# One PSUM tile per matmul bank, a transpose bank of its own, and batch 2 transposed on TensorE

## The chip, the core and the metric

The kernel runs on one core of a Trainium2 chip, as one launch. Of the core's engines it uses TensorE (PE: matmuls, with the weight loads shown apart as PEld), VectorE (DVE), ScalarE (ACT), a little GpSimd (POOL), and SyncE (SP), whose queue issues most DMAs. Matmul results go to PSUM, which has eight banks of 128 partitions x 512 float32; everything else stands in SBUF. The metric is the device time of one execution in microseconds. A profile is one execution of its own, with its own time.

## What is computed

```
def _attn_ref(q, k, v):                      # (8 batches, 8 heads, 576 tokens, 64)
    def phi(x, c, s):
        r = np.maximum(x, 0.0)
        return np.concatenate([r * c, r * s], axis=-1)
    q_p, k_p = phi(q, cos_w, sin_w), phi(k, cos_w, sin_w)   # cos, sin of the token's place
    kv = np.einsum('bhsf,bhsd->bhfd', k_p, v)
    z = np.sum(k_p, axis=2)
    num = np.einsum('bhsf,bhfd->bhsd', q_p, kv)
    den = np.einsum('bhsf,bhf->bhs', q_p, z)[..., None] + 1e-06
    return num / den
def _moe_ref(x, w_in, w_out):                # x (4608, 512), w_in (512, 2048), w_out (2048, 512)
    h = x @ w_in
    return (h * np.cos(h)) @ w_out
```

The attention's output, heads side by side, is x.

## The kernel before

**Attention, batch by batch.** `load` brings k, q and v of a batch into `raw` (km, qm, vm; one buffer each, so the next batch's load waits until this batch's was read). `prep` makes the two features of k and q with ReLU and a scale, one half on DVE, one on ACT (L236, L233), for five tiles t of 128 tokens; the fifth is half of one and is shared by two batches. `cast_v` makes v float16 (L249). `kv` sums kv and z of all heads into the two banks of the PSUM tile `ATT` (L257) and copies them to `kvz`. q must be transposed (feature by token): `q_pe` does it on TensorE into a PSUM bank, from which DVE or ACT copies it to `qT` (L288, L294, L292); `q_dma` does it with a DMA transpose from the SP queue (L298). Batches 0 and 1 take the first, the others the second way. `num` multiplies qT by kvz (L319); DVE takes the denominators (`den`), their reciprocals (`rec`) and the product x (L324, L327, L329). x is transposed in turn, by `x_pe` (L348, copied by ACT, L352) for the four whole tiles of batches 0 and 1 or by `x_dma` (L358), into `xT` or, for the shared tiles, `xR`.

**The two layers, in nine chunks of 512 tokens.** Chunk c is the whole tiles of batch c; chunk 8 is xR. `layer1` fills a PSUM bank with 4 (chunks 0 and 1: 8 of half the width) matmuls, 16 banks a chunk (L412, L395). For each bank ACT writes cos into `ch` (L368, one of four buffers) and DVE multiplies bank and ch into `gT` (L370). `layer2` sums 16 matmuls for each of four token tiles in a bank of M2 (L436); ACT copies it to `ost` (L448) and a DMA writes it out.

**PSUM.** The eight banks are four tiles of two banks: M1P[0], M1P[1] for layer 1 in turn, M2P for layer 2, and ATT. The early transposes and numerators borrow them as `PAIRS`. The profile and the orders below strip or number these: M is a tile of M1P or M2P.

**What sets the order.** Nothing is issued where it is written. Each step is recorded by `pl.add` with its engine, the time it is planned to occupy it, a due time and the keys that it reads and writes (a key is one bank, such as ("M1", 0)). `Plan.run` lists the steps by planned start and the functions are called in that order; each engine then runs its own instructions in that order. A DMA step occupies SP for its planned time and one shared wire for its bytes over its rate. The waits between engines are not the plan's: the framework adds them, and, as the orders below show, from the tiles that an instruction touches.

Of the kernel before, what the change touches and what calls it, by code (L numbers as in the profile page):

```python
# [11 lines left out]
ALU = mybir.AluOpType  # L12
# [87 lines left out]
def kernel(  # L100
# [41 lines left out]
    def sb(name, shape, dt=F16):  # L142
# [60 lines left out]
    def load(b, nm, due, hs=(slice(0, H),)):  # L203
        m, n = raw[nm], b % 2
        for i, h in enumerate(hs):
            five, four = tokens(src[nm][b][h])
            part = [(nm, hh) for hh in range(H)[h]]

            def go5(h=h, five=five):
                nc.sync.dma_start(out=blocks(m, n)[:, h], in_=five)  # L210

            def go4(h=h, four=four):
                nc.sync.dma_start(out=blocks(m, 1 - n)[:, h, 0:NT, :], in_=four)
# [3 lines left out]
            pl.add("SP", 0.62, 0, due, go4, (), [(x, 1 - n) for x in part],  # L217
                   dma=(nb * NT / 1e3, 330.0))
# [77 lines left out]
    def q_dma(b, t, due):  # L296
        dst, dkey = qdst(b, t)
        pl.add("SP", 0.62, 0, due, lambda: nc.sync.dma_start(  # L298
            out=dst, in_=qp[:, t].rearrange("p h g d -> p (h g d)"), transpose=True),
            [("qp", t, g, h) for g in range(2) for h in range(H)], [dkey],  # L300
            dma=(262.0, 200.0))

    xcount = [0]

    def num(b, t, due, pair=AT):
        A, *ak = pair
        n = xcount[0] % NX
        xcount[0] += 1
        parts = [(qdst(b, t)[0], kvz[b % 2])]
        rd = [qdst(b, t)[1]] + [("kvz", b % 2, i) for i in range(2)]  # L310
        if t == NT:
            parts.insert(0, (qT4[1 - b % 2], kvz[1 - b % 2]))
            rd += [("qT4", 1 - b % 2)] + [("kvz", 1 - b % 2, i) for i in range(2)]

        def mm():
            for h in range(H):
                hb, hh = divmod(h, HB)
                for i, (a, z) in enumerate(parts):
                    nc.tensor.matmul(  # L319
                        A[:, hb, hh * D1:(hh + 1) * D1], lhsT=a[:, h, :], rhs=z[:, h, :],  # L320
                        start=(i == 0), stop=(i == len(parts) - 1))
        pe(H * len(parts), MMA, due, mm, rd, ak)
        N = A[:, :, 0:HB * D1].rearrange("p b (h d) -> p b h d", h=HB)
        dve(0.08, due, lambda: nc.vector.tensor_scalar_add(  # L324
            out=den[n].rearrange("p (b h) -> p b h", b=2), in0=N[:, :, :, D], scalar1=1e-6),
            ak, [("den", n)])
        dve(0.12, due, lambda: nc.vector.reciprocal(out=rec[n], in_=den[n]),  # L327
            [("den", n)], [("rec", n)])
        dve(0.62, due, lambda: nc.vector.tensor_tensor(  # L329
            out=x16[n].rearrange("p (b h) d -> p b h d", b=2), in0=N[:, :, :, 0:D],  # L330
            in1=rec[n].rearrange("p (b h) -> p b h", b=2).unsqueeze(3).broadcast_to((P, 2, HB, D)),
            op=ALU.mult), ak + [("rec", n)], [("x16", n)])
        return n
# [7 lines left out]
    def x_pe(b, t, n, bank, key, eng, due):  # L341
# [8 lines left out]
        pe(NCT, MMT, due, mm, [("x16", n), "ID"], [key])  # L350
# [24 lines left out]
    def layer1(c):  # L375
# [29 lines left out]
        for j in range(NJT):  # L405
            m = m1n[0] % 4
# [17 lines left out]
    def layer2(c):  # L424
        G = gT[c % 2]
        NQ = 4
        for t in range(NT):
            m = m2n[0] % 2
# [29 lines left out]
            def put(dst, s, keys, q=nc.sync, eng="SP", nb=256.0):  # L458
                pl.add(eng, 0.62, 0, due + 1.0, lambda: q.dma_start(out=dst, in_=s), keys, [],
                       dma=(nb, 330.0))  # L460
# [7 lines left out]
            else:  # L468
                for n in range(2):
# [49 lines left out]
    def attention(b):  # L519
        T = start[b]  # L520
        if b == 0:
# [38 lines left out]
        for t in range(NT + 1):  # L560
# [10 lines left out]
        for t in ts:  # L571
            tt = T - 14 + 1.5 * t if t < NT else T
            if early and t < NT:
                pair = PAIRS[(0, 1, 3, 0)[t]]
                n = num(b, t, tt, pair)
                x_pe(b, t, n, pair[0][:, 0, :], pair[1], "ACT", tt)
            else:
                n = num(b, t, tt)
                x_dma(b, t, n, tt + 1)

    def late_q0():
        for g in range(2):
            prep(0, "q", NT, g, "DVE", 24, after=[("g", 0, 0, 0)])
        q_pe(0, NT, ATT[:, 0, :], ("ATT", 0), "ACT", 25)
# [48 lines left out]
```

## Time and profile before

| | |
|---|---|
| time, median of 3 runs (lowest, highest) | 350.78 us (350.75, 351.85) |
| the profiled execution | 350.4 us, of which the span from first to last instruction is 348.6 |
| granted TensorE clock, mean | 0.992 |
| DMA | 53.87 MB in 80217 packets, mean 155 GB/s |

The profile's rows are read so. A timeline row has start and length in us, engine, line of the source, operation, output<-inputs, how many instructions it merges, and in brackets the idle time before it and what ended it. A grouped row has, behind the count, busy us, the mean ns of one, then the idle us just before such instructions and what ended most of it. An instruction's length runs from its start to its last result; those that follow one another on an engine overlap, so a series can take less than the sum. A row of the chain of waits has start, length and what: the work that ended last, followed back from the end.

### The profile page before, as it was taken

The page shows a single profiled execution, that of the slowest core. Times are in us where ns is not written, and L with a number is a line of the kernel's source. Part 1 is how long each engine was busy: PE and PEld are TensorE (multiplying, and loading weights), DVE is VectorE, ACT ScalarE, POOL GpSimd, SP SyncE. Part 2 cuts the span into 40 slices and gives each one's busy share as a digit, 9 for nine tenths or more (in the row PEclk, how much of TensorE's full clock was granted, in tenths as well). Part 3 has the DMA queues.
Part 4 walks back from the last instruction along what each step waited for, and adds up shares of the span by engine and source line. Part 5 has one row for each costly group of instructions (what it writes and reads, how often), then busy time and mean ns, then how long its engine had stood idle before and what let it go on. Part 6 is the DMA issues. An engine that isn't in the chain of part 4 may idle for free.

```text
span 348.6 us, 5319 instructions
## 1 busy us (share of the span) xinstructions
PE 292.8 (84%) x2032; PEld 154.1 (44%) x2032; DVE 181.0 (52%) x387; ACT 179.2 (51%) x290; POOL 7.9 (2%) x19
## 2 busy tenths in 40 slices
PE   0478899676888779878988998999999999999983
PEld 0466646565543335433433453545444444444331
DVE  2646546967844667566666663643464333333300
ACT  2845558777553664564755665344433443443311
POOL 0430000000000000000000000000000000000000
PEclk9989999999999999999999999999999999999998
DMA  6999958999999989798494641561041010101111
GB/s 211 246 224 210 220 194 275 318 286 222 227 223 273 330 141 280 232 208 203 135 270 137 107 107 30 127 116 60 1 117 68 16 60 0 62 0 60 60 62 60
DMA packets 80217, 53.87 MB, mean 155 GB/s; under 512 B 48832, under 2 KB 77760, under 8 KB 80192
## 3 DMA queue, kind: packets, MB, share of 16 engines
q1 hardware_dynamic: 75520, 49.17, 53.3%
q0 software_dynamic: 4224, 4.19, 7.3%
q8 instruction: 16, 0.26, 0.3%
q10 hardware_dynamic: 448, 0.17, 0.2%
q14 instruction: 9, 0.07, 0.1%
HBM read 36.74 MB, written 9.44 MB: 132 GB/s over the span
## 4 chain that ended last, share of the span: by engine, by line
PE 57%; ACT 19%; DVE 12%; issue 6%; DMA 4%; SPq 0%; DVEq 0%; ACTq 0%
PE M L436 28%; PE M L412 20%; ACT ch L368 10%; DVE gT L370 10%; PE M L395 5%; DMA qm<-in_q_dram 4%; ACT ost L448 4%; ACT qp L233 2%; PE ATT L257 2%; PE ATT L319 1%; DVE x L329 1%; ACT V L246 1%; PE M L288 1%; ACT kp L233 1%; ACT qT L292 0%
## 5 line engine op out<-in xcount | busy, mean ns | idle before, releaser
L370 DVE TENSOR_TENSOR gT<-M,ch 128x512 f16<-128x512 f32 x144 | 98.2, 690 | 110.1 <-ACT ch L368 53.9
L368 ACT ACTIVATE ch<-M,PIH 128x512 f32<-128x512 f32 x144 | 96.6, 686 | 112.5 <-DVE gT L370 83.3
L436 PE MATMUL M<-w_out_sb,gT 128*128 128x512 f16 x576 | 141.0, 379 | 11.4 <-ACT ost L448 10.9
L412 PE MATMUL M<-xT,w_in_sb 128*128 128x512 f16 x384 | 94.7, 378 | 11.7 <-DVE gT L370 9.0
L436 PEld LDWEIGHTS <-gT 128*128 128x128 f16 x576 | 54.6, 97 | 76.7 <-issue 18.1
L412 PEld LDWEIGHTS <-w_in_sb 128*128 128x128 f16 x448 | 43.2, 97 | 68.2 <-issue 21.1
L395 PE MATMUL M<-xT,w_in_sb 128*128 128x256 f16 x256 | 30.4, 272 | 8.3 <-DVE gT L370 6.5
L448 ACT ACTIVATE ost<-M 128x512 f32<-128x512 f32 x35 | 20.6, 592 | 32.1 <-PE M L436 32.1
L395 PEld LDWEIGHTS <-w_in_sb 128*128 128x128 f16 x256 | 24.6, 97 | 13.1 <-issue 6.8
L233 ACT ACTIVATE kp<-km,CS 128x512 f16<-128x512 f32 x40 | 26.2, 712 | 4.9 <-DMA km<-in_k_dram 4.9
L233 ACT ACTIVATE qp<-qm,CS 128x512 f16<-128x512 f32 x39 | 26.2, 713 | 2.7 <-DMA qm<-in_q_dram 2.7
L236 DVE TENSOR_SCALAR kp<-km,CS 128x512 f16<-128x512 f32 x40 | 16.6, 481 | 11.3 <-DMA km<-in_k_dram 6.7
L329 DVE TENSOR_TENSOR x<-ATT,rec 128x512 f16<-128x512 f32 x30 | 20.6, 688 | 0.6
L319 PEld LDWEIGHTS <-qT 128*128 128x128 f16 x320 | 15.0, 101 | 10.1 <-issue 4.5
L236 DVE TENSOR_SCALAR qp<-qm,CS 128x512 f16<-128x512 f32 x41 | 18.1, 476 | 1.8 <-DMA qm<-in_q_dram 1.8
L288 PE MATMUL M<-IDENT,qp 128*128 128x128 f16 x72 | 6.3, 258 | 12.2 <-ACT qp L233 12.2
L412 PE MATMUL M<-xR,w_in_sb 128*128 128x512 f16 x64 | 16.4, 379 | 0.0
L319 PE MATMUL ATT<-kvz,qT 128*128 128x65 f16 x272 | 13.7, 195 | 2.0 <-DVE x L329 2.0
L249 DVE CAST V<-vm 128x512 f16<-128x512 f32 (+1 forms) x42 | 14.2, 382 | 0.0
L257 PE MATMUL ATT<-V,kp 128*128 128x65 f16 x320 | 11.8, 194 | 1.7 <-DVE V L249 1.0
L257 PEld LDWEIGHTS <-kp 128*128 128x128 f16 x320 | 11.1, 98 | 3.8 <-DVE V L249 1.2
L288 PEld LDWEIGHTS <-qp 128*128 128x128 f16 x80 | 6.2, 117 | 13.0 <-ACT qp L233 12.4
(38 smaller groups left out, 58.7 us busy)
## 6 DMA issues: line engine op xcount, KB each, us to landing
out_dram<-ost SPq DMA_DIRECT2D x32, 256.0 KB, 2.8
km<-in_k_dram SPq DMA_DIRECT2D x8, 640.0 KB, 5.3
qm<-in_q_dram SPq DMA_DIRECT2D x8, 640.0 KB, 5.7
km<-in_k_dram SPq DMA_DIRECT2D x8, 512.0 KB, 6.1
qm<-in_q_dram SPq DMA_DIRECT2D x8, 512.0 KB, 6.7
vm<-in_v_dram SPq DMA_DIRECT2D x6, 640.0 KB, 4.9
vm<-in_v_dram SPq DMA_DIRECT2D x6, 512.0 KB, 5.9
w_in_sb<-in_moe_w_in_dram POOLq DMA_DIRECT2D x4, 512.0 KB, 9.4
```

Of the source, the lines that this page charges most:

```text
L233: act(0.2 + 0.37 * f, due, lambda: nc.scalar.activation(out=out_, in_=in_, func=AF.Relu, scale=sc), rd, wr)
L236: dve(0.09 + 0.28 * f, due, lambda: nc.vector.tensor_scalar(out=out_, in0=in_, scalar1=0.0, scalar2=sc, op0=ALU.max, op1=ALU.mult), rd, wr)
L257: nc.tensor.matmul(ATT[:, hb, hh * D1:(hh + 1) * D1], lhsT=kp[:, t, h].rearrange("p g d -> p (g d)"), rhs=V1[b % 2][:, t, h, :], start=(t ...
L288: nc.tensor.matmul(ps[:, h, :], lhsT=qp[:, t, h].rearrange("p g d -> p (g d)"), rhs=IDENT, is_transpose=True)
L319: nc.tensor.matmul(A[:, hb, hh * D1:(hh + 1) * D1], lhsT=a[:, h, :], rhs=z[:, h, :], start=(i == 0), stop=(i == len(parts) - 1))
L329: dve(0.62, due, lambda: nc.vector.tensor_tensor(out=x16[n].rearrange("p (b h) d -> p b h d", b=2), in0=N[:, :, :, 0:D], in1=rec[n].rearra ...
L368: act(0.59, due, lambda: nc.scalar.activation(out=ch[c], in_=bank, func=AF.Sin, bias=PIH, scale=1.0), [key, "PIH"], [("ch", c)])
L370: dve(0.61, due, lambda: nc.vector.tensor_tensor(out=dst, in0=bank if len(dst.shape) == 2 else bank.rearrange("p (j s) -> p j s", j=dst.sh ...
L395: nc.tensor.matmul(M1[m][:, jj * 2 * P:(jj + 1) * 2 * P], lhsT=w_in_sb[:, cc, j * P:(j + 1) * P], rhs=X[:, cc, ts], start=(cc == 0), stop= ...
L412: nc.tensor.matmul(M1[m], lhsT=w_in_sb[:, cc, j * P:(j + 1) * P], rhs=X[:, cc, :], start=(cc == 0), stop=(cc == NCT - 1))
L436: nc.tensor.matmul(M2[m], lhsT=G[:, j, t * P:(t + 1) * P], rhs=w_out_sb[:, j, :], start=(j == 0), stop=(j == NJT - 1))
L448: act(0.5, due, lambda O=O, t=t, m=m: nc.scalar.activation(out=O[:, t % 2, :], in_=M2[m], func=AF.Copy), [("M2", m)], [("ost", o, t % 2, 0)])
```

## The change

Each bank of M1 and M2 becomes a PSUM tile of its own: three for layer 1 instead of four, two for layer 2, and the eighth bank, TR, serves transposes. ATT stays a tile of two banks. `num` runs as two halves, each on one bank, and where it borrows two tiles DVE takes den and x in two instructions. Batch 2's five q tiles and the x tiles of batch 2, with the shared one of batch 1, go over TensorE and TR in place of the DMA. In the plan an SP transpose now occupies SP for 1.25 and has a lower rate, and loads have 310 for 330.

```diff
-    M1P = [ppool.tile([P, 2, SM], F32, name=f"M1_{n}") for n in range(2)]
-    M2P = ppool.tile([P, 2, Dm], F32, name="M2")
+    NM1, NM2 = 3, 2
+    M1 = [ppool.tile([P, SM], F32, name=f"M1_{n}") for n in range(NM1)]
+    M2 = [ppool.tile([P, Dm], F32, name=f"M2_{n}") for n in range(NM2)]
+    TR = ppool.tile([P, SM], F32, name="TR")
     ATT = ppool.tile([P, 2, SM], F32, name="ATT")
-    M1 = [M1P[n // 2][:, n % 2, :] for n in range(4)]
-    M2 = [M2P[:, n, :] for n in range(2)]
-    BANKS = [(M1[n], ("M1", n)) for n in range(4)]
     HALVES = (slice(0, HB), slice(HB, H))
-    AT = (ATT, ("ATT", 0), ("ATT", 1))
-    PAIRS = [(M1P[0], ("M1", 0), ("M1", 1)), (M1P[1], ("M1", 2), ("M1", 3)),
-             (M2P, ("M2", 0), ("M2", 1)), AT]
-
+    BANKS = [(M1[n], ("M1", n)) for n in range(NM1)] + [(TR, ("TR", 0))]
+    BANKS2 = [(M2[n], ("M2", n)) for n in range(NM2)]
+    PAIRS = [(BANKS[0], BANKS[1]), (BANKS2[0], BANKS2[1]), None, (BANKS[2], BANKS[3])]
+
+    Q_PE, X_PE = range(2, 3), range(1, 3)
...
+            queue, eng, occ = nc.sync, "SP", 0.65
...
-            pl.add("SP", 0.62, 0, due, go5, (), [(x, n) for x in part],
-                   dma=(nb * (NT + 1) / 1e3, 330.0))
...
+            pl.add(eng, occ, 0, due, go5, (), [(x, n) for x in part],
+                   dma=(nb * (NT + 1) / 1e3, 310.0))
...
     def q_dma(b, t, due):
         dst, dkey = qdst(b, t)
-        pl.add("SP", 0.62, 0, due, lambda: nc.sync.dma_start(
+        pl.add("SP", 1.25, 0, due, lambda: nc.sync.dma_start(
             out=dst, in_=qp[:, t].rearrange("p h g d -> p (h g d)"), transpose=True),
             [("qp", t, g, h) for g in range(2) for h in range(H)], [dkey],
-            dma=(262.0, 200.0))
+            dma=(262.0, 160.0))
...
-    def num(b, t, due, pair=AT):
-        A, *ak = pair
+    def num(b, t, due, pair=None):
         n = xcount[0] % NX
         xcount[0] += 1
+        bank = [p[0] for p in pair] if pair else [ATT[:, hb, :] for hb in range(2)]
+        keys = [p[1] for p in pair] if pair else [("ATT", 0), ("ATT", 1)]
...
-        def mm():
-            for h in range(H):
-                hb, hh = divmod(h, HB)
+        def mm(hb):
+            for hh in range(HB):
+                h = hb * HB + hh
                 for i, (a, z) in enumerate(parts):
                     nc.tensor.matmul(
-                        A[:, hb, hh * D1:(hh + 1) * D1], lhsT=a[:, h, :], rhs=z[:, h, :],
+                        bank[hb][:, hh * D1:(hh + 1) * D1], lhsT=a[:, h, :], rhs=z[:, h, :],
                         start=(i == 0), stop=(i == len(parts) - 1))
...
+        for hb in range(2):
+            pe(HB * len(parts), MMA, due, lambda hb=hb: mm(hb), rd, [keys[hb]])
+        if pair is None:
+            N = [ATT[:, :, 0:HB * D1].rearrange("p b (h d) -> p b h d", h=HB)]
+            cut = [(slice(0, H), 2, keys)]
+        else:
+            N = [x[:, 0:HB * D1].rearrange("p (b h d) -> p b h d", b=1, h=HB) for x in bank]
+            cut = [(HALVES[hb], 1, [keys[hb]]) for hb in range(2)]
+        dk = [("den", n, i) for i in range(len(cut))]
+
+        def split(ap, k):
+            return ap.rearrange("p (b h) ... -> p b h ...", b=k)
+        for A, (hs, k, ks), d in zip(N, cut, dk):
+            dve(0.06 + 0.01 * k, due, lambda A=A, hs=hs, k=k: nc.vector.tensor_scalar_add(
+                out=split(den[n][:, hs], k), in0=A[:, :, :, D], scalar1=1e-6), ks, [d])
+        dve(0.12, due, lambda: nc.vector.reciprocal(out=rec[n], in_=den[n]), dk, [("rec", n)])
+        for A, (hs, k, ks) in zip(N, cut):
+            dve(0.08 + 0.27 * k, due, lambda A=A, hs=hs, k=k: nc.vector.tensor_tensor(
+                out=split(x16[n][:, hs, :], k), in0=A[:, :, :, 0:D],
+                in1=split(rec[n][:, hs], k).unsqueeze(3).broadcast_to((P, k, HB, D)),
+                op=ALU.mult), ks + [("rec", n)], [("x16", n, i) for i in range(2) if k == 2 or hs == HALVES[i]])
...
     def x_dma(b, t, n, due):
         dst, dkey = xdst(b, t)
-        pl.add("SP", 0.62, 0, due, lambda: nc.sync.dma_start(
+        pl.add("SP", 1.25, 0, due, lambda: nc.sync.dma_start(
             out=dst, in_=x16[n].rearrange("p h d -> p (h d)"), transpose=True),
-            [("x16", n)], [dkey], dma=(131.0, 200.0))
+            [("x16", n, 0), ("x16", n, 1)], [dkey], dma=(131.0, 140.0))
...
-            m = m1n[0] % 4
+            m = m1n[0] % NM1
...
-            m = m2n[0] % 2
+            m = m2n[0] % NM2
...
             for t in range(NT):
-                A, key, _ = PAIRS[t]
                 n = num(b, t, 7 + t, PAIRS[t])
-                x_pe(b, t, n, A[:, 0, :], key, "ACT", 7 + t)
+                x_pe(b, t, n, *BANKS[t], "ACT", 7 + t)
...
             if early:
                 q_pe(b, t, *BANKS[t % 4], "ACT" if t % 2 else "DVE", tt + 1)
+            elif b in Q_PE:
+                q_pe(b, t, TR, ("TR", 0), "ACT" if t % 2 else "DVE", tt + 1)
             else:
                 q_dma(b, t, tt + 1)
...
             if early and t < NT:
-                pair = PAIRS[(0, 1, 3, 0)[t]]
-                n = num(b, t, tt, pair)
-                x_pe(b, t, n, pair[0][:, 0, :], pair[1], "ACT", tt)
+                n = num(b, t, tt, PAIRS[(0, 2, 3, 0)[t]])
+                x_pe(b, t, n, *BANKS[(0, 2, 2, 0)[t]], "ACT", tt)
             else:
                 n = num(b, t, tt)
-                x_dma(b, t, n, tt + 1)
+                if b in X_PE:
+                    x_pe(b, t, n, TR, ("TR", 0), "ACT", tt)
+                else:
+                    x_dma(b, t, n, tt + 1)
...
-        q_pe(0, NT, ATT[:, 0, :], ("ATT", 0), "ACT", 25)
+        q_pe(0, NT, TR, ("TR", 0), "ACT", 25)
```

What the plan makes of it stands in three places. The first is layer 1 of the last chunk. On DVE, the products before:

```order
L370 TENSOR_TENSOR gT1_98<-M1_0_106,ch0_99 128x512 [waits PE_49,Activation_49]
L370 TENSOR_TENSOR gT1_98<-M1_0_106,ch1_100 128x512 [waits Activation_49]
L370 TENSOR_TENSOR gT1_98<-M1_1_107,ch2_101 128x512 [waits PE_49,Activation_49]
L370 TENSOR_TENSOR gT1_98<-M1_1_107,ch3_102 128x512 [waits Activation_49]
L370 TENSOR_TENSOR gT1_98<-M1_0_106,ch0_99 128x512 [waits PE_49,Activation_49]
```

and now:

```order
L383 TENSOR_TENSOR gT1_98<-M1_1_107,ch0_99 128x512 [waits Activation_49]
L383 TENSOR_TENSOR gT1_98<-M1_2_108,ch1_100 128x512 [waits Activation_49]
L383 TENSOR_TENSOR gT1_98<-M1_0_106,ch2_101 128x512 [waits Activation_49]
L383 TENSOR_TENSOR gT1_98<-M1_1_107,ch3_102 128x512 [waits Activation_49]
L383 TENSOR_TENSOR gT1_98<-M1_2_108,ch0_99 128x512 [waits Activation_49]
```

M1_0_106 was a pair of banks and is now one bank. The first product of each pair waited for PE as well as for ACT (Activation); now none does. On ACT, the cosines there before:

```order
L368 ACTIVATE ch0_99<-M1_0_106,PIH_63 128x512 [waits PE_49,Activation_49]
L368 ACTIVATE ch1_100<-M1_0_106,PIH_63 128x512 [waits DVE_49]
L368 ACTIVATE ch2_101<-M1_1_107,PIH_63 128x512 [waits PE_49,Activation_49]
L368 ACTIVATE ch3_102<-M1_1_107,PIH_63 128x512 [waits DVE_49]
L448 ACTIVATE ost2_105<-M2_108 128x512 [waits DMAHW6_49,DMAHW5_49,PE_49]
```

and now:

```order
L381 ACTIVATE ch0_99<-M1_1_107,PIH_63 128x512 [waits DVE_49,PE_49]
L381 ACTIVATE ch1_100<-M1_2_108,PIH_63 128x512 [waits DVE_49,PE_49]
L381 ACTIVATE ch2_101<-M1_0_106,PIH_63 128x512 [waits DVE_49,PE_49]
L381 ACTIVATE ch3_102<-M1_1_107,PIH_63 128x512 [waits DVE_49,PE_49]
L461 ACTIVATE ost1_104<-M2_1_110 128x512 [waits PE_49]
```

The second cosine of a pair waited for DVE alone, that is for the product of the pair's first bank; each one now waits for its own matmuls on PE, and for DVE to have read its ch buffer four banks ago.

The second place is ACT ahead of chunk 1. Before (xT1 are copies of chunk 1's x, qp the preparation of batch 2's q, whose first waits for its load):

```order
L352 ACTIVATE xT1_95<-M1_1_107 128x4x128 [waits DVE_49,PE_49]
L352 ACTIVATE xT1_95<-ATT_109 128x4x128 [waits DVE_49,PE_49]
L352 ACTIVATE xT1_95<-M1_0_106 128x4x128 [waits DVE_49,PE_49]
L233 ACTIVATE qp_73<-qm_70,CS_61 128x8x64 [waits DMAHW1_49,DMAHW0_49,Activation_49]
L233 ACTIVATE qp_73<-qm_70,CS_61 128x8x64 [waits Activation_49]
L352 ACTIVATE xT1_95<-M1_0_106 128x4x128 [waits DVE_49,PE_49]
L233 ACTIVATE qp_73<-qm_70,CS_61 128x8x64 [waits Activation_49] x2
L275 ACTIVATE kvz0_80<-ATT_109 128x520 [waits DVE_49,PE_49]
L233 ACTIVATE qp_73<-qm_70,CS_61 128x8x64 [waits Activation_49]
L368 ACTIVATE ch0_99<-M1_0_106,PIH_63 128x512 [waits PE_49]
```

and now:

```order
L365 ACTIVATE xT1_95<-M1_2_108 128x4x128 [waits DVE_49,PE_49]
L365 ACTIVATE xT1_95<-M1_0_106 128x4x128 [waits DVE_49,PE_49]
L235 ACTIVATE qp_73<-qm_70,CS_61 128x8x64 [waits DMAHW1_49,DMAHW0_49,Activation_49]
L235 ACTIVATE qp_73<-qm_70,CS_61 128x8x64 [waits Activation_49]
L277 ACTIVATE kvz0_80<-ATT_112 128x520 [waits DVE_49,PE_49]
L365 ACTIVATE xT1_95<-M1_2_108 128x4x128 [waits DVE_49,PE_49]
L365 ACTIVATE xT1_95<-M1_0_106 128x4x128 [waits DVE_49,PE_49]
L235 ACTIVATE qp_73<-qm_70,CS_61 128x8x64 [waits Activation_49] x3
L365 ACTIVATE xR_96<-TR_111 128x4x128
L381 ACTIVATE ch0_99<-M1_1_107,PIH_63 128x512 [waits DVE_49,PE_49]
```

Two of the four copies of chunk 1's x stand behind batch 2's q, where one did, and the copy of the shared tile (xR) has come in ahead of the first cosine.

The third place is the SP queue from the load of batch 3's v on. Before:

```order
L210 DMA vm_71<-in_v_dram 64x8x320
L213 DMA vm_71<-in_v_dram 64x8x256
L358 DMA_TRANSPOSE xR_96<-x16_0_90 128x4x128
L298 DMA_TRANSPOSE qT0_74<-qp_73 128x8x128
L298 DMA_TRANSPOSE qT1_75<-qp_73 128x8x128
L298 DMA_TRANSPOSE qT2_76<-qp_73 128x8x128
L298 DMA_TRANSPOSE qT3_77<-qp_73 128x8x128
L298 DMA_TRANSPOSE qT4_0_78<-qp_73 128x8x128
L210 DMA qm_70<-in_q_dram 64x8x320
```

and now:

```order
L212 DMA vm_71<-in_v_dram 64x8x320
L215 DMA vm_71<-in_v_dram 64x8x256
L212 DMA qm_70<-in_q_dram 64x8x320
L215 DMA qm_70<-in_q_dram 64x8x256
L212 DMA km_69<-in_k_dram 64x8x320
L215 DMA km_69<-in_k_dram 64x8x256
```

Batch 2's transposes are gone from the queue, and the loads of the next batches follow one another.

More of the change, by code (lines that the diff above doesn't have):

```diff
@@ L207, in load, with go5, go4 @@
             part = [(nm, hh) for hh in range(H)[h]]
[L209 to L213, printed above, removed]
+            queue, eng, occ = nc.sync, "SP", 0.65
+            def go5(h=h, five=five, queue=queue):
+                queue.dma_start(out=blocks(m, n)[:, h], in_=five)
+            def go4(h=h, four=four, queue=queue):
+                queue.dma_start(out=blocks(m, 1 - n)[:, h, 0:NT, :], in_=four)
             nb = len(part) * R * D * 4
-            pl.add("SP", 0.62, 0, due, go5, (), [(x, n) for x in part],
-                   dma=(nb * (NT + 1) / 1e3, 330.0))
-            pl.add("SP", 0.62, 0, due, go4, (), [(x, 1 - n) for x in part],
-                   dma=(nb * NT / 1e3, 330.0))
+            pl.add(eng, occ, 0, due, go5, (), [(x, n) for x in part],
+                   dma=(nb * (NT + 1) / 1e3, 310.0))
+            pl.add(eng, occ, 0, due, go4, (), [(x, 1 - n) for x in part],
+                   dma=(nb * NT / 1e3, 310.0))
     def hk(nm, hs=range(H)):
@@ L476, in layer2 @@
                             put(five[:, NT, fs], blocks(O, n)[:, t % 2, fs],
-                                [("ost", o, t % 2, f)], *((nc.scalar, "ACT") if f == 0 else ()), nb=65.0)
+                                [("ost", o, t % 2, f)], *((nc.scalar, "ACT") if f == 0 else (nc.sync, "SP")), nb=65.0)
     def setup():
```

17 lines of the change are left out of this document (3 added, 14 removed).

## The prediction

> **What bounds the kernel now.** I read the page's busy shares first.
>
> ```profile
> span 348.6 us, 5319 instructions
> ...
> PE 292.8 (84%) x2032; PEld 154.1 (44%) x2032; DVE 181.0 (52%) x387; ACT 179.2 (51%) x290; POOL 7.9 (2%) x19
> ```
>
> TensorE (PE) is the busiest engine, but a busy PE is not a PE at its peak, so the page alone does not say how much room is left. For that I count its matmuls from the start of chunk 1 on (67.7 us), with the grouped view of that stretch, and set beside them what each kind takes when nothing stops it, from the chain of waits (start, us, what).
>
> ```profile
> L436 PE MATMUL M<-w_out_sb,gT 128*128 128x512 f16 x512 | 126.1, 379 | 10.6 <-ACT ost L448 10.2
> L412 PE MATMUL M<-xT,w_in_sb 128*128 128x512 f16 x384 | 94.7, 378 | 11.7 <-DVE gT L370 9.0 <-ACT ch L368 2.5
> L412 PE MATMUL M<-xR,w_in_sb 128*128 128x512 f16 x64 | 16.4, 379 | 0.0
> L395 PE MATMUL M<-xT,w_in_sb 128*128 128x256 f16 x128 | 15.1, 272 | 4.8 <-DVE gT L370 4.2 <-ACT ch L368 0.5
> L319 PE MATMUL ATT<-kvz,qT 128*128 128x65 f16 x240 | 12.0, 193 | 2.0 <-DVE x L329 2.0
> L257 PE MATMUL ATT<-V,kp 128*128 128x65 f16 x240 | 8.2, 193 | 0.0
> ```
>
> ```profile
> 86.44 2.79 PE M L395 x24
> 167.31 1.21 PE ATT L257 x40
> 298.86 0.86 PE M L412 x4
> 341.22 2.77 PE M L436 x12
> ```
>
> Four 512-column matmuls take 0.86 us, so one takes 0.216; a 256-column one 2.79/24 = 0.116; a 65-column one 1.21/40 = 0.030. The work is 960 x 0.216 + 128 x 0.116 + 480 x 0.030 = 207.4 + 14.9 + 14.4, with four transposes 237 us. PE's last matmul ends at 341.22 + 2.77 = 344.0, and chunk 1 starts at 67.8 (a row further down): 276.2 us for 237 us of work. **PE stands idle for 39 us of it**, and 4.6 us follow the last matmul. Who holds it up? The view of waits (engine line waited for: total us, times, longest) over the whole span:
>
> ```profile
> ACT ch L368 <- DVE gT L370: 83.3, 53, 2.2
> DVE gT L370 <- PE M L412: 52.7, 36, 2.7
> PE M L436 <- ACT ost L448: 10.9, 20, 0.9
> ```
>
> No data explains the first: L368 on ScalarE (ACT) reads a matmul bank and fills ch, and L370 on VectorE (DVE) reads both; the cosine of one bank needs no product of another. The timeline of one cycle late in the run, where there is no attention work, shows what happens.
>
> ```profile
> 291.17 1.03 PE L412 MATMUL M<-xT,w_in_sb 128*128 128x512 f16 x4
> 292.30 0.69 DVE L370 TENSOR_TENSOR gT<-M,ch 128x512 f16<-128x512 f32 x1 [1.81 <-PE M L412]
> 293.03 0.69 ACT L368 ACTIVATE ch<-M,PIH 128x512 f32<-128x512 f32 x1 [2.19 <-DVE gT L370]
> 293.75 0.69 DVE L370 TENSOR_TENSOR gT<-M,ch 128x512 f16<-128x512 f32 x1 [0.75 <-ACT ch L368]
> 297.84 1.02 PE M L436 x4
> 305.37 1.02 PE M L436 x4
> ```
>
> The product of a pair's first bank waits for the matmuls of its second (292.30 behind 291.17 + 1.03), the cosine of the second waits for that product, and the next matmuls of the pair wait for the last product. The two banks share one tile, and the program's waits, shown with the change, are of the tile. The last two rows (from the chain) are one cycle apart: 7.53 us for 32 matmuls, which are 8 x 0.863 = 6.90 of work.
>
> **The change, part by part.** (1) *One tile per bank* removes those waits: in the new order no product waits for PE. The interleaved cycle leaves 12 matmuls (2.6 us) of slack: three M1 banks at 1.73 us each are 5.18 us, and one bank needs 1.03 + 0.69 + 0.69 and three handoffs of some 0.06 by the rows above, 2.6. M2 gets two tiles, so L436 no longer waits for the other half's copy (10.9 us in all). What is late next is PE itself: at most the 39 us go.
>
> (2) *The start of chunk 1* moves with it. Rows of the timeline (the second is the chain's), and the landing row of batch 1's v:
>
> ```profile
> 23.59 1.03 PE L395 MATMUL M<-xT,w_in_sb 128*128 128x256 f16 x8
> 43.09 4.33 PE M L436 x20
> ...
> 40.65 1.20 SPq L210 DMA_DIRECT2D vm<-in_v_dram  x1
> DMA to landing us min/median/max: 7.9/8.2/8.5
> 53.47 0.60 ACT L448 ACTIVATE ost<-M 128x512 f32<-128x512 f32 x1 [2.38 <-PE M L436]
> 53.97 2.55 ACT L233 ACTIVATE qp<-qm,CS 128x512 f16<-128x512 f32 x4
> 60.54 0.63 SPq L213 DMA_DIRECT2D qm<-in_q_dram  x1
> 67.77 1.04 PE L395 MATMUL M<-xT,w_in_sb 128*128 128x256 f16 x8
> 68.13 1.34 ACT L233 ACTIVATE qp<-qm,CS 128x512 f16<-128x512 f32 x2 [2.36 <-DMA qm<-in_q_dram]
> 72.17 2.41 ACT L368 ACTIVATE ch<-M,PIH 128x512 f32<-128x512 f32 x4
> ```
>
> Batch 1's loads do not move: all of it has landed by about 50 (40.65 + 1.20 + 8). Its q preparation on ACT does: it stood behind the copy at 53.47, which waited for PE. Chunk 0's layer 1 (16 groups of 8 from 23.6 to 43.1, 19.5 us for a work of 16 x 0.93 = 15) should end some 3 to 4 us earlier and layer 2 lose its 0.69 stall, so that copy comes 4 to 5 us earlier, and with it the release of raw q and batch 2's q load (60.54, landing 68). In the new order ACT and DVE still hold part of chunk 1's last inputs behind that landing. I put chunk 1's first matmul at 64.0, between 62.3 (the copy's whole 5.5) and 67.8 (the load bound after all).
>
> (3) *Batch 2 transposed on PE.*
>
> ```profile
> 60.74 0.61 PE L288 MATMUL M<-IDENT,qp 128*128 128x128 f16 x8
> 61.45 0.69 DVE L294 COPY qT<-M 128x1024 f16<-128x1024 f16 x1 [0.80 <-PE M L288]
> L288 PE MATMUL M<-IDENT,qp 128*128 128x128 f16 x72 | 6.3, 258 | 12.2 <-ACT qp L233 12.2
> L292 ACT ACTIVATE qT<-M 128x1024 f16<-128x1024 f16 x4 | 4.0, 1018 | 0.9 <-DVE qT L294 0.9
> L352 ACT ACTIVATE xT<-M 128x512 f16<-128x512 f16 x6 | 3.6, 593 | 4.5 <-PE M L348 4.4
> 70.95 10.15 SPq L298 DMA_TRANSPOSE qT<-qp  x5
> ```
>
> Five q steps of eight and four x steps of four come behind chunk 1's start (the fifth x step, batch 1's remainder, ahead of it): 56 x 0.61/8 = 4.3 us of PE. ACT gets 2 x 1.02 + 5 x 0.59 = 5.0 us, DVE 3 x 0.69 = 2.1; the SP queue loses ten transposes, of which five took 10.15 us. PE's 4.3 are on the path and I count them; the copies have cover, since each of ACT and DVE is busy for about half the span. The page "TensorE: Matmul & The Clock Gate" of the Trainium skill (Part 4: PE-mode transpose) gives about 275 ns for a 128x128 transpose inside a kernel; by it the 56 would cost 15.4 us and the total 333. The 0.61 us row for eight speaks against it here, since they overlap.
>
> (4) *Planned costs and split steps.* The planned 1.25 for an SP transpose alters only the order. The split of numerators into halves adds, for six steps, one den (0.16 in the row below) and some overhead of a second product each, all before chunk 1: in part (2)'s bounds. Three banks for four is in (1).
>
> (5) *What idleness stays.* In chunk 1, ACT has 16 cosines, ten preparations, two qT and four xT copies. At the pitch of the 72.17 row (0.60 each) and with (3)'s copies that is 26 x 0.60 + 2.0 + 2.4 = 20.0 us, beside a PE work of 14.9 + 4.3 + 8 x 0.216 + 32 x 0.030 = 21.9: nearly equal, with all nine transposes going through one bank, TR. I take 4.5 us idle, between 2 and 10. In the six later chunks with attention, the numerator steps are tight on DVE:
>
> ```profile
> 202.36 0.69 DVE L370 TENSOR_TENSOR gT<-M,ch 128x512 f16<-128x512 f32 x1 [0.75 <-ACT ch L368]
> 202.97 0.16 DVE L324 TENSOR_SCALAR den<-ATT 128x8 f32<-128x8 f32 x1
> ...
> 203.40 0.69 DVE L329 TENSOR_TENSOR x<-ATT,rec 128x512 f16<-128x512 f32 x1
> ```
>
> From 202.36 to 204.09 is 1.73 us, exactly the 8 matmuls between two such steps. I take 1.0 us a chunk, 6, between 0.25 (the four steps' handoffs) and 2.5 (a preparation behind each). For transposes landing late, 1, between 0 and 3. Idle in all: 11.5, from 3.5 to 28.
>
> **Sum.** PE's work from chunk 1: 237 + 4.3, less 40 x 0.030 (batch 2's kv now runs ahead of it) and the 0.3 that had stood for four transposes: 239.9. Then 64.0 + 239.9 + 11.5 + 4.6 = 320.0 us of span. The profiled execution took 350.4 us with 348.6 of span, 1.8 outside it (and 0.4 under the median of 350.78): **321.8 us**.
>
> **Rivals.** *B, DVE and ACT are late next*: each numerator step carries a preparation or cast, 2 us a chunk; chunk 1 loses 9, landings 2: idle 23, so 333. For it: the 1.73 row; against it: both engines are half idle.
> *P, transposes cost PE their single duration*: the group row has 258 ns as the mean of one q transpose, so 56 x 0.258 = 14.4 and the time is 332. Against it: 72 of them kept PE busy for 6.3 us, 0.088 each. The Trainium skill's 275 ns would be this.
> *C, the change doesn't do what it says*: cosines still name DVE among their waits in the new order. That wait is for ch, four banks back. If it was the one that came last, idle stays 39 and time is 67.8 + 239.9 + 39 + 4.6 + 1.8 = 353; with (2)'s gain, 349. Against it: products wait for PE, which ch cannot explain.
> *D, slower: the ring of three banks is too short.* Where layer 1 runs alone, three banks give 2.6/3 = 0.87 us a bank against PE's 0.86, with no slack; interleaved, slack is 2.6. A chunk has 15 foreign ACT instructions (ten preparations, four copies, kvz) of 0.63; if every one stopped PE, 9.5 us a chunk, 57 in six: 373. It ends slower once 29 us come back, five a chunk beyond my one, nine or ten of the fifteen. Against it: a stop needs more than four of them inside one turn of a bank.
>
> **How the numbers follow.** Forecast 0.76, B 0.16, P 0.02, C 0.03, D 0.03. The forecast's own range is 312 (62.3 + 239.9 + 3.5 + 4.6 + 1.8) to 330; nine tenths of it lie there, 0.68. Up to 335 come P and two thirds of B: 0.81, so 312 to 335. A measurement tells 0.3%, about 1 us, from no change. Faster: forecast, B and P, 0.94; same: most of C, 0.02; slower: D and the rest of C, 0.04.
>
> **What would show it.** Right: the cosine's wait on gT falls from 83 us to a few, and the product's on layer-1 matmuls to nothing; the late cycle is 6.9 us for 32 matmuls; PE's last 64 matmuls run without the three gaps for ost; chunk 1 starts near 64. Wrong: chunk 1 at 67 or later, with q of batch 2 in its chain (part 2); PE waiting for x or den in most numerator steps (B); steps of eight q transposes taking over 1 us (P); PE waiting for gT in the late cycles (C, D).

## The result, and the profile after

The changed kernel took **312.45 us** (median of 4 runs, 311.55 to 313.73), beside 351.31 us for the kernel before on the same chip: a ratio of 0.889, 95% interval 0.884 to 0.894. The forecast was 321.8 with a range of 312 to 335, so the direction and the mechanism came out, and the fall was 9 us larger than forecast, at the very edge of the range. The profiled execution took 311.55 us. One execution of run e12 below, the profiled one, took 348.88 us at a granted clock of 0.846, so that run's row has its time alone.

The page of the changed kernel, first lines:

```profile
span 309.8 us, 5467 instructions
...
PE 284.9 (92%) x2092; PEld 158.2 (51%) x2092; DVE 183.0 (59%) x402; ACT 185.9 (60%) x297; POOL 7.9 (3%) x19
```

Its PE groups from the start of chunk 1 (65.37) on. The last column is the idle time just before the group, and its releaser:

```profile
L449 PE MATMUL M<-w_out_sb,gT 128*128 128x512 f16 x512 | 127.6, 379 | 0.0
L425 PE MATMUL M<-xT,w_in_sb 128*128 128x512 f16 x384 | 96.9, 379 | 0.0
...
L408 PE MATMUL M<-xT,w_in_sb 128*128 128x256 f16 x128 | 15.4, 272 | 0.0
...
L290 PE MATMUL TR<-IDENT,qp 128*128 128x128 f16 x40 | 3.0, 218 | 1.5 <-DVE qT L296 0.8 <-ACT xR L365 0.5 <-ACT qT L294 0.2
```

Before, the three large groups had 10.6, 11.7 and 4.8 us of idle time ahead of them, named for ost, gT and ch; now they have none. Only the transposes through the single bank TR still wait, 1.5 us in all. The waits of the whole span:

```profile
DVE gT L383 <- ACT ch L381: 76.8, 84, 3.1
ACT ch L381 <- PE M L425: 60.6, 75, 2.5
ACT ch L381 <- DVE gT L383: 15.3, 15, 1.3
ACT ost L461 <- PE M L449: 15.1, 26, 2.9
```

The pattern has turned round: 83.3 us of cosines waiting for products are 15.3, products no longer wait for PE, and ACT and DVE now wait in the natural order, cosine for matmul and product for cosine. They wait because PE is the slowest: it is busy for the whole of the next window. The windows of 130 to 200 us (length, then busy time and count of PE, PEld, DVE, ACT, POOL, clock, DMA share, GB/s), after and before:

```profile
130.00:200.00 70.00, 70.00 (x490) 35.06 (x489) 49.55 (x109) 44.26 (x71) 0.00 (x0) 1.00 0.81 194
```

```profile
130.00:200.00 70.00, 59.71 (x402) 28.61 (x401) 44.40 (x99) 39.77 (x64) 0.00 (x0) 1.00 0.78 197
```

In the same 70 us PE runs 490 matmuls where it ran 402. The end of the chain of waits of the changed kernel:

```profile
34.87 5.24 PE M L408 x48
...
242.50 0.86 PE M L449 x4
243.36 0.86 PE M L425 x4
...
290.85 14.69 PE M L449 x68
```

Groups of four follow at 0.86 us without a gap, and the last 68 matmuls run at 14.69/68 = 0.216 with no ost gap among them.

**The account used below.** PE work is each shape's count times its pitch when nothing stops it: 1024 x 0.216 (the last row above), 256 x 0.109 (5.24/48), 640 x 0.030 (the prediction's row), and 128-column transposes at 0.056 (measured below). Span less work is PE's idle time. Before: 274.6 of work (112 transposes), so 74.0 idle. After: 277.9 (172), so 31.9 idle. The idle falls by 42.1, the work grows by 3.3, and the span falls by 38.8. By the starts of the matmuls in the trace, 34.6 of the idle before lay ahead of the end of chunk 1's layer 1, 34.7 behind it and 4.8 in the tail; after, these are 27.2, 0.3 and 4.4. So **from 87 us up to the tail PE has nothing left to lose**, and what remains is the start-up. Idle time so counted includes what a lower clock cost: in a few stretches of the start-up the granted clock was 0.5, which by the starts of the matmuls lost 1.1 us before and 1.2 after, but 2.5 in e3, 3.9 in e10, 4.7 in e2 and 5.1 in e5 below.

### The profile page after: what moved, and what is told of

Same layout as the page of the kernel before. It is cut to its first block, busy times and chain, and to the rows that moved or that the text cites. A ratio compares the mean times of both kernels' runs of the same rounds, so it can differ in the third digit from the quotient of the medians.

```text
span 309.8 us, 5467 instructions
## 1 busy us (share of the span) xinstructions
PE 284.9 (92%) x2092; PEld 158.2 (51%) x2092; DVE 183.0 (59%) x402; ACT 185.9 (60%) x297; POOL 7.9 (3%) x19
## 4 chain that ended last, share of the span: by engine, by line
PE 85%; DVE 5%; ACT 4%; DMA 2%; issue 1%; SPq 0%; DVEq 0%; ACTq 0%
PE M L449 39%; PE M L425 31%; PE M L408 7%; PE ATT L259 3%; PE ATT L322 3%; DMA qm<-in_q_dram 2%; DVE x L342 2%; PE M L290 1%; ACT ch L381 1%; ACT kp L235 1%; ACT qp L235 1%; DVE V L251 1%; DVE qp L238 1%; PE TR L290 0%; PE TR L361 0%
## 5 line engine op out<-in xcount | busy, mean ns | idle before, releaser
L381 ACT ACTIVATE ch<-M,PIH 128x512 f32<-128x512 f32 x144 | 98.5, 692 | 80.4 <-PE M L425 60.6
L449 PE MATMUL M<-w_out_sb,gT 128*128 128x512 f16 x576 | 142.6, 379 | 0.0
L425 PE MATMUL M<-xT,w_in_sb 128*128 128x512 f16 x384 | 96.9, 379 | 0.0
L322 PEld LDWEIGHTS <-qT 128*128 128x128 f16 x320 | 14.3, 98 | 6.7 <-issue 1.0
L290 PEld LDWEIGHTS <-qp 128*128 128x128 f16 x120 | 8.9, 111 | 15.2 <-ACT qp L235 12.2
L290 PE MATMUL M<-IDENT,qp 128*128 128x128 f16 x56 | 4.9, 259 | 12.2 <-ACT qp L235 12.2
L259 PE MATMUL ATT<-V,kp 128*128 128x65 f16 x320 | 13.3, 202 | 2.5 <-DVE x L342 1.7
L259 PEld LDWEIGHTS <-kp 128*128 128x128 f16 x320 | 12.6, 103 | 5.2 <-issue 2.7
```

The lines of the kernel that those rows point to most:

```text
L259: nc.tensor.matmul(ATT[:, hb, hh * D1:(hh + 1) * D1], lhsT=kp[:, t, h].rearrange("p g d -> p (g d)"), rhs=V1[b % 2][:, t, h, :], start=(t ...
L322: nc.tensor.matmul(bank[hb][:, hh * D1:(hh + 1) * D1], lhsT=a[:, h, :], rhs=z[:, h, :], start=(i == 0), stop=(i == len(parts) - 1))
L381: act(0.59, due, lambda: nc.scalar.activation(out=ch[c], in_=bank, func=AF.Sin, bias=PIH, scale=1.0), [key, "PIH"], [("ch", c)])
L425: nc.tensor.matmul(M1[m], lhsT=w_in_sb[:, cc, j * P:(j + 1) * P], rhs=X[:, cc, :], start=(cc == 0), stop=(cc == NCT - 1))
L449: nc.tensor.matmul(M2[m], lhsT=G[:, j, t * P:(t + 1) * P], rhs=w_out_sb[:, j, :], start=(j == 0), stop=(j == NJT - 1))
```

## The experiments

Each kernel is the changed one with one edit, except the first, which is the kernel before with one edit. Ratios are to the kernel before on the same chip.

| run | median us | ratio, 95% interval | span | PE idle | chunk 1's first matmul |
|---|---|---|---|---|---|
| before | 351.31 | 1 | 348.6 | 74.0 | 67.8 |
| after | 312.45 | 0.889 (0.884 to 0.894) | 309.8 | 31.9 | 65.4 |
| e1_split_alone | 313.36 | 0.892 (0.889 to 0.896) | 310.9 | 36.3 | 62.0 |
| e2_pairs_back | 354.50 | 1.010 (1.006 to 1.013) | 352.5 | 74.6 | 77.6 |
| e5_m1_pairs | 346.85 | 0.987 (0.984 to 0.991) | 344.9 | 67.0 | 77.2 |
| e6_m2_pair | 318.99 | 0.910 (0.905 to 0.914) | 317.0 | 39.1 | 67.3 |
| e3_batch2_dma | 309.43 | 0.880 (0.877 to 0.882) | 307.1 | 32.5 | 65.4 |
| e4_old_costs | 315.97 | 0.898 (0.895 to 0.901) | 313.8 | 35.9 | 64.7 |
| e8_ring4 | 312.83 | 0.889 (0.887 to 0.892) | 310.0 | 32.1 | 63.8 |
| e11_x_first | 311.98 | 0.887 (0.884 to 0.889) | 309.2 | 31.3 | 62.4 |
| e12_dma_x_first | 309.39 | 0.879 (0.876 to 0.882) | | | |
| e7_ring2 | 313.19 | 0.891 (0.887 to 0.895) | 310.6 | 32.7 | 64.7 |
| e10_double_x | 319.64 | 0.909 (0.906 to 0.913) | 317.6 | 39.7 | 66.6 |
| e9_all_pe | 328.70 | 0.934 (0.931 to 0.937) | 326.8 | 32.5 | 66.1 |

### The split alone

```diff
-    M1P = [ppool.tile([P, 2, SM], F32, name=f"M1_{n}") for n in range(2)]
-    M2P = ppool.tile([P, 2, Dm], F32, name="M2")
+    M1 = [ppool.tile([P, SM], F32, name=f"M1_{n}") for n in range(4)]
+    M2 = [ppool.tile([P, Dm], F32, name=f"M2_{n}") for n in range(2)]
```

(den and product of the early numerators are issued in halves, in place.)

> The kernel before, every step in its place, with four M1 tiles and two M2 tiles of one bank each; batch 2 still goes through DMA transposes and the planned costs are the old ones. Theory (the shared tiles held PE up): the cosine's wait on gT falls from 83 us to under 6, PE's idle from chunk 1 on from 39 us to between 4 and 12 (what batch 2's DMA transposes leave), chunk 1 starts at 64 to 67; time 315 to 326 us, nearest 320. Rival (a good part of the gain comes from the new order and from batch 2 on PE): the waits go but PE idles over 15 us on other things, time 330 to 345. Rival C (the waits were for ch, not for the tile): within 3 us of 350.

313.36 us, a little below the theory's range: the split alone brings 38 of the 39 us. The cosine's wait on gT falls to 8.3 us, not under 6, and chunk 1 starts at 62.0, ahead of the expected 64. PE idles 8.4 us behind chunk 1's start, and the view of PE's waits names the largest piece of it besides the start-up:

```profile
PE M L416 <- DMA xT<-x: 4.9, 4, 2.4
```

Those are DMA transposes that land after the order had planned them.

### The pairs put back

```diff
-    M1 = [ppool.tile([P, SM], F32, name=f"M1_{n}") for n in range(NM1)]
+    M1P = [ppool.tile([P, 2, SM], F32, name=f"M1_{n}") for n in range(2)]
+    M1 = [M1P[n // 2][:, n % 2, :] for n in range(NM1)]
-    M2 = [ppool.tile([P, Dm], F32, name=f"M2_{n}") for n in range(NM2)]
+    M2P = ppool.tile([P, 2, Dm], F32, name="M2")
+    M2 = [M2P[:, n, :] for n in range(NM2)]
-    TR = ppool.tile([P, SM], F32, name="TR")
+    TR = M1P[1][:, 1, :]
```

Both pairs (e2), M1's and TR's lines alone (e5), M2's lines alone (e6):

> The changed kernel, every step in its place, with M1 banks 0 and 1 in one tile, M1 bank 2 and TR in another, and both M2 banks in a third. Theory: the gains of the split go and with three M1 banks, of which one shares its tile with TR alone, a little less than all of it comes back: cosine waits on gT 40 to 80 us in all, time 338 to 353, nearest 345. Rival (order and PE transposes made the gain): under 325.

> The changed kernel, every step in its place, M1 banks 0 and 1 in one tile and bank 2 with TR in another; M2's two banks stay apart. Theory: most of the false waits are M1's (cosine on product), M2's are 10.9 us of which some lie beside them: time 332 to 345, nearest 338. Rival (M2's copies are what stops PE, since PE's largest waits by name in the kernel before are on ost): under 322.

> The changed kernel, every step in its place, with both M2 banks in one tile again. Theory: 0.5 us of PE at every change of bank where ost's copy must end before the other bank may be written, for 30 of 36 half rows at most: 20 x 0.5 = 10 us, time 318 to 326, nearest 321. Rival: the planner has put the copies where PE works on layer 1, so that the tile's second wait costs PE nothing while M1 is split: within 2 us of 312.5.

354.5, 346.9 and 319.0: the first two ended 1.5 and 1.9 us above the theory's ranges, the third inside, and the rivals fell. Paired M1, with TR, costs 34.4 us, paired M2 6.5, both 42.1, so they nearly add up. With both pairs PE idles 74.6 us, as in the kernel before (74.0). The 3 us by which e2 is the slower are about what its 60 added transposes cost; that it is only they is not shown, since e2's profiled execution also lost 3.6 us more to the clock. The waits of e5, then of e6:

```profile
ACT ch L382 <- DVE gT L384: 67.6, 47, 2.4
...
PE M L409 <- ACT ch L382: 6.3, 7, 1.3
PE M L426 <- ACT ch L382: 6.0, 9, 1.4
PE M L426 <- DVE gT L384: 4.2, 5, 1.6
```

```profile
PE M L450 <- ACT ost L462: 4.8, 9, 0.7
```

The cosine's long wait returns with the shared tile and not with its order, and matmuls wait for cosines and products of the other bank; in e6 the copy to ost is the one large wait of PE that is new.

### Batch 2 by DMA, and the planner's costs

```diff
-    Q_PE, X_PE = range(2, 3), range(1, 3)
+    Q_PE, X_PE = (), ()
```

> The changed kernel with batch 2 and batch 1's remainder transposed by DMA again; single-bank tiles, three M1 banks, TR and the new planned costs stay. In the run with the split alone chunk 1 started at 62.0 and PE idled 8.5 us behind it; in the changed kernel 65.4 and 2.4. Theory (PE transposes trade 4 us of PE work for the landing waits of DMA transposes): start still near 65 (the order on PE ahead of chunk 1 is the same), idle 6 to 10, PE work 3.5 less; time 312.5 to 318, nearest 315. Rival (PE transposes are worth nothing, the DMA ones were hidden): idle under 4, time under 311.

309.43 us: the theory fell and the rival was right. Without the PE transposes the kernel is **3.0 us faster** than the changed one (the intervals of the ratios do not meet). The idle is about the same (32.5 against 31.9, with 1.3 us more lost to the clock), the work 3.3 less, and no wait of PE in e3 names a DMA transpose. The transposes on PE save nothing here; they are added work.

```diff
-            queue, eng, occ = nc.sync, "SP", 0.65
+            queue, eng, occ = nc.sync, "SP", 0.62
-        pl.add("SP", 1.25, 0, due, lambda: nc.sync.dma_start(
+        pl.add("SP", 0.62, 0, due, lambda: nc.sync.dma_start(
-            dma=(262.0, 160.0))
+            dma=(262.0, 200.0))
```

(and 140 to 200 for x, 310 to 330 for loads, 0.65 to 0.62 for stores)

> The changed kernel with the planner's old costs (0.62 us for every issue on SP, transposes at 200 a unit, loads at 330). Theory: the costs move a few steps only; from batch 3 on DMA transposes are planned earlier than they land, so that numerators stand in PE's order ahead of data: idle 2 to 6 us more, time 312 to 318, nearest 314. Rival: no difference, within 1 us of 312.5, since PE has work queued ahead of every numerator.

315.97 us, in the theory's range: the old costs lose 3.5 us, again with intervals that do not meet. PE's waits now name landings, 2.3 us of them:

```profile
PE M L425 <- DMA qT<-qp: 1.7, 1, 1.7
...
PE M L425 <- DMA xT<-x: 0.6, 1, 0.6
```

So the new costs remove late landings such as the split alone had left; with them, DMA transposes arrive in time and need no help from PE. Of the rest of its added idle, 1.1 us is clock (2.3 lost against 1.2). Which of the planned costs does it was not separated.

### The price of a PE transpose

```diff
-    Q_PE, X_PE = range(2, 3), range(1, 3)
+    Q_PE, X_PE = range(2, 8), range(1, 8)
```

> The changed kernel with the transposes of batches 3 to 7 on PE too: 292 more 128x128 transposes (200 for q, 92 for x), 48 DMA transposes fewer, and 48 more copies out of TR on ACT and DVE. Theory (on a PE that never waits a transpose costs its pitch, 0.054 to 0.076 us, and saves nothing): 16 to 22 us more, time 327 to 336, nearest 330. Rival P (each costs its single duration of 0.258 us, or the Trainium skill's 275 ns, page TensorE: Matmul & The Clock Gate, Part 4): 75 to 80 us more, 385 or above. Third case (copies out of one bank TR stop PE): 340 to 360.

328.70 us, 16.25 more for 292 transposes: **0.056 us each**, as the theory had it; P fell. The grouped view of e9 from 88 us on:

```profile
L290 PE MATMUL TR<-IDENT,qp 128*128 128x128 f16 x200 | 15.2, 219 | 0.0
...
L361 PE MATMUL TR<-IDENT,x 128*128 128x128 f16 x92 | 8.9, 219 | 0.0
```

219 ns is the mean of one, 15.2/200 = 0.076 a share of busy time that runs on into the next group, and 0.056 what it costs in the span. The trace says the same by itself: behind each of the 292 the next matmul starts 0.055 to 0.056 us later. So nothing is left for the 48 added copies on ACT and DVE: PE idles 32.5 us.

### How much slack the numerators have

```diff
-            dve(0.08 + 0.27 * k, due, lambda ...: nc.vector.tensor_tensor(
+            dve(0.08 + 0.27 * k, due, lambda ...: [nc.vector.tensor_tensor(
...
-                op=ALU.mult), ks + [("rec", n)], ...
+                op=ALU.mult) for _ in range(2 if b > 2 else 1)], ks + [("rec", n)], ...
```

> The changed kernel, every step in its place, with each numerator's product on DVE done twice in batches 3 to 7: 23 more DVE instructions of 0.69 us, which give the same values. Theory (a numerator step has slack of a ring's turn behind it: PE idles 0.3 us in all the later chunks): PE idles at most 3 us more, time 312.5 to 315.5. Rival (the steps are tight, 1.73 us of DVE work for 8 matmuls of 1.73 us, as the prediction priced them): every extra product stops PE for 0.5 to 0.69 us, 12 to 16 us, time 324 to 329.

319.64 us, 7.2 more: between the two, so neither theory had the slack right. Two numerator steps of the changed kernel (timeline):

```profile
195.45 0.68 DVE L383 TENSOR_TENSOR gT<-M,ch 128x512 f16<-128x512 f32 x1
...
195.93 0.42 PE L322 MATMUL ATT<-kvz,qT 128*128 128x65 f16 x8
...
196.39 0.17 DVE L338 TENSOR_SCALAR den<-ATT 128x8 f32<-128x8 f32 x1 [0.26 <-PE ATT L322]
196.59 0.20 DVE L340 RECIPROCAL rec<-den 128x8 f32<-128x8 f32 x1
196.82 0.69 DVE L342 TENSOR_TENSOR x<-ATT,rec 128x512 f16<-128x512 f32 x1
...
197.43 0.68 DVE L383 TENSOR_TENSOR gT<-M,ch 128x512 f16<-128x512 f32 x1
...
197.91 0.42 PE L322 MATMUL ATT<-kvz,qT 128*128 128x65 f16 x8
```

and the same place with the product doubled:

```profile
199.77 0.68 DVE L383 TENSOR_TENSOR gT<-M,ch 128x512 f16<-128x512 f32 x1
199.91 0.42 PE L322 MATMUL ATT<-kvz,qT 128*128 128x65 f16 x8 [0.22 <-DVE x L342]
...
200.80 1.42 DVE L342 TENSOR_TENSOR x<-ATT,rec 128x512 f16<-128x512 f32 x2
...
202.13 0.68 DVE L383 TENSOR_TENSOR gT<-M,ch 128x512 f16<-128x512 f32 x1
202.27 0.42 PE L322 MATMUL ATT<-kvz,qT 128*128 128x65 f16 x8 [0.22 <-DVE x L342]
```

In the changed kernel a step takes 1.98 us (195.93 to 197.91): eight matmuls of 0.216 and the numerator's own eight of 0.030, together 1.97. PE sets it, and DVE stands idle for 0.26 of it. Doubled, the step takes 2.36 us, 0.38 longer: DVE goes from gT to den without a gap, and PE waits for the product before the next numerator may write ATT. DVE's own series and the loop through ATT (numerator, den, rec, products) end together here, so which of the two binds is not separated. The view of PE's waits has:

```profile
PE ATT L322 <- DVE x L342: 3.0, 13, 0.4
```

The view names 13 numerators; by the starts of the matmuls 15 of them lost 5.9 us and two kv, which write ATT too, another 0.8. That is the whole of the 6.6 by which PE's idle behind chunk 1's layer 1 grew (0.3 to 6.9). The 1.2 more that lie ahead of it are not the doubling's, which begins with batch 3: this execution lost 2.7 us more to the clock there.

### The ring of M1 banks

```diff
-            m = m1n[0] % NM1
+            m = m1n[0] % 2
```

(e8: a ring of four, with TR as the fourth bank)

> The changed kernel with a ring of two M1 banks for layer 1 (the third stays for batch 1's steps). Theory (the slack of the ring is what hides numerators and preparations): two banks give 2 x 1.73 = 3.45 us for a turn that needs 2.6, so that two foreign instructions in one turn stop PE; and layer 1 alone (chunk 0) falls to 1.3 us a bank from 0.9: start 2 to 5 us later, idle behind it 8 to 20 us in place of 2.4; time 320 to 335, nearest 326. Rival (even two banks are enough, as long as each is its own tile): under 316.

> The changed kernel with a ring of four banks for layer 1: TR is its fourth bank, and the transposes of batch 2 take turns with layer 1 in it. Theory: with three banks PE loses 2 us in chunk 1 and nothing after 82 us, so that a fourth bank can win 2 us at most behind the start of chunk 1 and 1 to 2 us in chunk 0's layer 1, and the shared bank may lose as much: 309 to 314. Rival (three banks just suffice in this order; a fourth moves the order, and transposes stop layer 1): 315 or more.

313.19 and 312.83 us: two, three or four banks give the same time within the intervals. For two banks the theory fell; for four it held. Chunk 0's layer 1 starts its last matmul 4 us later with two (43.8 against 39.8), but the idle up to the end of chunk 1's layer 1 is 28.0 against 27.2: the start-up waits for other things.

### The start of chunk 1

In the changed kernel (timeline) batch 2's kv stands on PE ahead of the last three x steps of batch 1, and waits on DVE:

```profile
59.63 1.73 DVE L251 CAST V<-vm 128x512 f16<-128x512 f32 x5
...
62.28 2.36 PE L259 MATMUL ATT<-V,kp 128*128 128x65 f16 x40 [1.73 <-DVE x L342]
...
62.90 1.34 ACT L235 ACTIVATE qp<-qm,CS 128x512 f16<-128x512 f32 x2 [2.68 <-DMA qm<-in_q_dram]
...
65.37 1.36 PE L408 MATMUL M<-xT,w_in_sb 128*128 128x256 f16 x11
```

The edit (e12 has it too, with batch 2 by DMA):

```diff
-            tt = T - 14 + 1.5 * t if t < NT else T
+            tt = (T - 14 if b > 1 else T - 30) + 1.5 * t if t < NT else T
```

> The changed kernel with the due times of batch 1's numerators and x transposes 16 us earlier, so that on PE chunk 1's first matmuls stand ahead of batch 2's kv, and on DVE batch 1's x ahead of batch 2's casts of v. Theory (in the changed kernel chunk 1 starts 3.4 us later than with the split alone because kv of batch 2, which waits for those casts, stands ahead of the last transposes): chunk 1 starts at 61.5 to 63.5, time 309 to 311.5. Rival (the start is set by batch 2's q load, which lands at 62.9 and holds up ACT): start stays at 65, time 312 to 313.

> The changed kernel with batch 2 and batch 1's remainder transposed by DMA (as in the run that took 309.4) and batch 1's numerators and x transposes due 16 us earlier (as in the run whose chunk 1 started at 62.4). Theory (the two gains lie in different places and add up): start 62 to 63, PE work behind it 235.6, idle 2.5 to 3.5, tail 4.8; time 306 to 309, nearest 307.4. Rival (with chunk 1 earlier, batch 2's DMA transposes land too late for its numerators): idle 5 to 7, time 309.5 to 312.

In e11 the start moved as the theory said, to 62.40, but the time did not: 311.98, within the interval of the changed kernel. In e12 it was 309.39 where 307.4 was expected, between theory and rival. The timeline of e11 shows why for the first:

```profile
62.40 1.03 PE L408 MATMUL M<-xT,w_in_sb 128*128 128x256 f16 x8 [0.68 <-ACT xT L365]
63.27 0.39 PE L361 MATMUL M<-IDENT,x 128*128 128x128 f16 x4
...
64.36 1.37 PE L259 MATMUL ATT<-V,kp 128*128 128x65 f16 x40
```

kv and two x steps only changed places with the first matmuls of chunk 1; the idle up to the end of chunk 1's layer 1 is 26.6 instead of 27.2. The rows hold one more thing: kv's 40 matmuls took 2.36 us in the changed kernel and 1.37 here. The granted clock was 0.51 from 61.5 to 65.0 there, and 1.00 here; e11's own stretch at 0.50 came earlier, from 22.6 to 26.0. As times the two edits of e12 do add up: the earlier start brought nothing clear of noise in e11, and it brings nothing beside e3's 309.43.

## Why the prediction was right, and where its sizes were off

**What bounds the kernel** was right: 39 us of idle PE came from waits of shared tiles. The split alone gave 38 of the 39 us that the time fell by, and the pairs put back took them away in the same order.

**(1) One tile per bank** was right, as was "what is late next is PE itself". The ring of three has more slack than the forecast gave it: even two banks suffice. M2's tile, with 10.9 us of waits by name, was worth 6.5 us (e6). Of the signs, the product's wait on PE is gone, the late groups follow at 0.86 us, which is 6.9 for 32 matmuls, and the gaps for ost are gone; the cosine's wait on gT is 15.3 us, more than the few that were expected, but PE does not wait for it.

**(2) The start of chunk 1** came at 65.4, not 64.0 (and at 66.6 in e10, whose order is the same up to there), inside its bounds of 62.3 to 67.8. Of the 1.4 us, up to 1.2 were lost to the clock just ahead of it, a term that the forecast did not have. It was a weak mark: e11 moved it by 3.0 us and the time stayed.

**(3) The transposes** were priced at 4.3 us; 56 x 0.056 = 3.1. That the copies have cover held. The step never asked what the DMA transposes had cost, and with the new planned costs the answer is nothing: this part of the change is a loss of 3.0 us.

**(4) The planned costs** were put into the bounds of (2), as a change of order alone. They are worth 3.5 us, of which 2.3 are seen as landings that PE no longer waits for. The errors of (3) and (4) have opposite signs: DMA transposes with the old costs (e1) and PE transposes with the new ones end within 1 us of each other.

**(5) What idleness stays** is the term that was mis-sized, and it holds nearly all of the 9 us: **11.5 us were forecast, about 2.4 measured** (2.1 in chunk 1, where 4.5 stood; 0.3 in the six later chunks and for late transposes, where 7 stood). From 65.37 to 305.54 (290.85 + 14.69) are 240.2 us, which at the forecast's own unit prices, 239.9 of work, would leave 0.3 of idle; that work was 2.3 too high (0.9 by 0.116 for 0.109 in chunk 1's layer 1, 1.2 by the transposes, the rest by rounding: 237 + 4.3 - 1.2 - 0.3 is 239.8). The step that failed is "1.73 us, exactly the 8 matmuls between two such steps": it left out the numerator's own eight matmuls, which give DVE another 0.24 us. With them PE, not DVE, sets the step, as the timeline shows, and doubling the product shows how thin that margin is. The 4.5 of chunk 1 was an estimate without a row that measures it; 2.1 lies at the low end of its 2 to 10.

**Sum**: the start 1.4 later, work 2.3 less, idle 9.1 less, the tail 4.3 for 4.6, make 10.3 off a span of 320.0, which is 309.7 beside the measured 309.8. That the time lies inside the range, by 0.45 us, is luck: the idle of 2.4 is below the 3.5 from which the lower end was made, the later start made up for it, and two of the four executions, the profiled one among them, lie under 312.

**Rivals.** B (DVE and ACT late next) did not occur, though a numerator step is only 0.26 us from it. P fell in e9, C in e1 and e5, D in e7.

## What to carry to other kernels

Give every bank that is filled and drained on its own a tile of its own: a wait for a tile is a wait for its latest use, whichever bank that was, and here three tiles of two banks (two in M1, one in M2) cost a PE-bound kernel 42 us. Test a change of several parts apart: here one part brought nearly all, one a little, and one cost 3 us under the cover of the others; **the changed kernel without its PE transposes (309.4 us) beats both kernels**. To see whether an engine is tight in a cycle, count all of the bounding engine's work in it, the small matmuls too, and judge a change of order by the total idle of that engine, not by when one instruction starts.

## What the runs showed of the hardware

A 128x128 transpose among other matmuls costs PE 0.056 us in the span, though the profile gives each a length of 219 ns. The page "TensorE: Matmul & The Clock Gate" of the Trainium skill (Part 4: PE-mode transpose) has about 275 ns in one kernel's context and says that the full clock does not engage for transpose mode. As a price that figure does not hold here, where they overlap with their neighbours, and PE's clock (the number ahead of the DMA share) is full in e9's window with the most of them, 128 among 561 matmuls; no run here has a long stretch of transposes alone:

```profile
130.00:200.00 70.00, 70.00 (x561) 38.36 (x558) 47.12 (x98) 50.80 (x82) 0.00 (x0) 1.00 0.36 115
```

The start of chunk 1 came at 65.4 (the changed kernel) and 66.6 (e10) in two executions with the same order up to there. The clock lines of their pages, tenths of the full clock in 40 equal slices of the span (9 is 90% or more), show what differed, the changed kernel first:

```profile
PEclk9999999989999999999999999999999999999999
```

```profile
PEclk9968999989999999999999999999999999999998
```

Both have a stretch at half the clock just ahead of chunk 1 (0.51 from 61.5 to 65.0, and 0.51 from 63.0 to 66.5). e10 has another, 0.50 from 18.7 to 25.5, where the changed kernel had 1.00, and by the starts of its matmuls PE lost 2.4 us in it. So a start that is read from one execution can be off by more than 1 us with no change in the kernel. What sets such a stretch off was not tested.
